# Fused linear attention and MLP on one core: loads of a pair's first sets reordered, attention steps of two shapes side by side, ranks laid out anew

## Chip, cores and metric

The kernel runs on one core of one Trainium2 chip. Times are device microseconds (us) of that core for one execution of the whole program. All engines of the core work on it: PE (matmuls), PEld (its weight loads), DVE, ACT, POOL and SP, whose queue issues nearly all DMAs in order.

## What is computed

```python
def phi(x):                       # random features of a row, 128 of them
    h = np.einsum('bhsd,md->bhsm', x, omega) - np.sum(x*x, -1, keepdims=True)/2
    return np.exp(h - np.max(h, -1, keepdims=True)) / np.sqrt(m)
q_p, k_p = phi(q*scale), phi(k*scale)
kv  = einsum('bhsm,bhsd->bhmd', k_p, v);  z = sum(k_p, axis=2)
num = einsum('bhsm,bhmd->bhsd', q_p, kv); den = einsum('bhsm,bhm->bhs', q_p, z)[..., None] + 1e-06
x   = (num/den) as [8, 576, 512]          # 8 batches, 8 heads of 64, 576 rows
xn  = (x - mean)/sqrt(var + 1e-06) * g_ln
out = x + np.maximum(xn @ w_ch1, 0) @ w_ch2   # 512 -> 2048 -> 512
```

## The kernel before

**Tiles.** The 4608 rows of x are 36 chunks of 128 (`c`), and four chunks make a tile of 512 rows (`t`, 9 of them). The MLP of tiles 0 to 2 (`NREG`) is done tile by tile (`mm1` L1073 to L1075, `mm2` L1116 to L1118). Tiles 3 to 8 are done in three pairs (`gen_pair`, p = 0, 1, 2): the two tiles of a pair are the halves of one larger product that is computed with 7 products where 8 would be needed (`one_set`, products of `product` at L1374 to L1376). Each float32 product is made of three matmuls of 128x512 on high and low parts; such a matmul is called a wide matmul below.

**A pair** has four groups. A group is two sets of 7 products (`one_set(p, j)`, j = 0 to 7; one product is 6 wide matmuls) and then 8 chunks of the second layer (`one_chunk`, L1466 to L1468, 12 wide matmuls each). The seven left-hand forms of the activations (`gen_forms`, names `A11, S3, S2, A12, S1, A22, S4`, products 0 to 6) are made once per pair by ACT (L1292) and DVE (L1295, L1302) from the transposed, normalized x of both tiles. The forms of pairs 1 and 2 go into the buffers of the pair before, which come free in its last set.

**Loads of a pair,** all from DRAM by SP's queue: the weights of each product, 256 KB (`gen_slot`, L1343, a ring of 8 slots `w<-wf`; product m's slot is filled again for product m + 8); the second layer's weights, 512 KB for each of 16 f, four buffers (`gen_w2`, L1359, `w<-w2a`); and the pair's 8 chunks of x for the residual, 256 KB each (`gen_back`, L933, `x<-away`), to which each chunk's result is added (`drain`, L1485). Finished chunks are stored by L1148.

**Attention** runs between the MLP's matmuls, ahead of the tiles that need it. A step holds a pair of PSUM banks and is one of three shapes: "row" steps, K = 64, 8 matmuls of 64x128 or 2 of 64x512 (keys L651, early queries L812); "col" steps, 16 matmuls onto 64 columns (sums of keys and values L714, numerators L895); "all" steps, which have the MLP's own shape (later queries L829, L830). Row and col steps are called narrow. Between two wide matmuls there can be a visit of one or more narrow steps. After L895 a chunk of x is normalized (L906, L979), split (L996), transposed by a DMA (L999) and copied to the pair's forms' source.

**Order.** The whole order of work is written out by a planner (`Plan`) that keeps a modelled clock for each engine. Every generator part has a rank; among parts that can start, the lowest rank goes first. `serve` decides at each wide matmul whether a visit is made. With `lend` (between chunks and between sets) it looks for two narrow steps of the same shape, which then go back to back on two bank pairs; a third may join as a guest. A single narrow step is taken when its rank has fallen below `plan.at`, the rank of the MLP's present place, or when it has waited for over `PATIENCE`. If the MLP itself is blocked, any visit is made (`run`). `EARLIER` gives the attention of each tile its rank, `WF` that of the weights' forms and their stores, `SHIFT` moves single parts.

Of the kernel before, what the change touches and what calls it, by code (L numbers as in the profile page):

```python
# [39 lines left out]
TC = T // P  # L40
NREG = 3
# [32 lines left out]
class Plan:  # L74
# [14 lines left out]
    FILL, IDLE = 10000, 20000  # L89
    HOLDER = 100  # L90
    LENT = 1500
    SWITCH = 0.37
    PATIENCE = 50.0
    PEEK, AHEAD, TILL = {ACT: 0.1, DVE: 0.1, PE: 0.1}, 5, 60.0
    BIAS = {PE: 0.0, ACT: 0.2, DVE: 0.5, POOL: -0.2, SP: 0.0}
# [3 lines left out]
    def __init__(self):  # L99
        self.free_at = dict.fromkeys((PE, ACT, DVE, POOL, SP), 0.0)  # L100
        self.dma_at, self.landed = 0.0, [0.0] * Plan.QUEUE
        self.lock, self.two_at = (0.0, 0.0), 0.0
        self.free_at[SP] = 0.74
        self.ready = []
        self.blocked = []
        self.made = {}
        self.places = {}
        self.cur = None
        self.count = 0
        self.visits = []  # L110
        self.mlp = None
        self.pair, self.loan, self.at = (), (), 0
        self.shared = {}

    def add(self, rank, gen):
# [76 lines left out]
    def serve(self, lend):  # L192
# [6 lines left out]
        if lend and len(narrow) > 1 and self.open(self.loan):  # L199
            pairs = [(a, b) for i, a in enumerate(narrow) for b in narrow[i + 1 :] if a.want[1] == b.want[1]]  # L200
            if pairs:
                a, b = pairs[0]
                guests = [p for p in narrow if p not in (a, b) and p.want[1] == a.want[1] == "col" and p.want[3]]
                if not guests and a.want[1] == "col":
                    third = [p for p in narrow if p not in (a, b) and p.want[1] == "col"]
                    if third and b.want[3]:
                        b, guests = third[0], [b]
                    elif third and a.want[3]:
                        a, guests = third[0], [a]
                if guests:  # L210
                    self.lodge(guests[0])
                    self.go(b, self.loan, b.want[2])
                    self.go(a, self.pair, a.want[2])
                    return True
                self.go(b, self.loan, Plan.SWITCH + b.want[2])
                self.go(a, self.pair, a.want[2])
                return True
        for p in waiting:
            if p.want[1] == "all":
                if len(narrow) < 2:  # L220
                    self.go(p, self.pair, p.want[2])
                    return False
            elif p.rank < self.at or now - p.ready(PE) > Plan.PATIENCE:
                self.go(p, self.pair, Plan.SWITCH + p.want[2])
                return False
        return False
# [85 lines left out]
def favor_ffn(ctx, tc, kT, kTr, vF, vR, qT, qD, omT, gT, w1, w2, out):  # L312
# [1042 lines left out]
    def gen_w2(p, f, t_w):  # L1355
        w = tile_of(t_w, [P, 2, DM], F32R)
        yield wait("w2", f)
        yield dma(2 * P * DM)
        nc.sync.dma_start(f32(w), w2_away[f])  # L1359
        w2s[p, f] = t_w, w  # L1360
        done(("w2s", p, f))
# [18 lines left out]

    def one_set(p, j):

        ta, f, g = NREG + 2 * p, 2 * j, 2 * j + 1
        b_a, b_d = b_h
        b_b, b_c = b_acc[0:2] if j % 2 == 0 else b_acc[1::-1]
        sk = snaps[j % 2]
        yield "get", (b_a,)
        yield from product(p, j, 0, b_a, True)
        plan.add(MOST_URGENT, gen_copy(p, j, b_a, b_b))
        yield "get", (b_d,)  # L1390
        yield from product(p, j, 1, b_d, True)
        yield wait("a2b", p, j)
        yield from product(p, j, 2, b_b, False)
        plan.add(MOST_URGENT, gen_snap(p, j, b_b, sk[0], 0))
        plan.add(MOST_URGENT, gen_x2(p, j, b_c, b_d, sk[0]))
        yield from product(p, j, 3, b_a, False)
        plan.add(MOST_URGENT, relu2(ta, f, bank(b_a), b_a))
        yield wait("snap", p, j, 0)
        yield from product(p, j, 4, b_b, False)
        plan.add(MOST_URGENT, gen_snap(p, j, b_b, sk[1], 1))  # L1400
        plan.add(MOST_URGENT, gen_y2(p, j, b_d, sk[1], ta + 1, g))
        yield wait("x2", p, j)
        yield from product(p, j, 5, b_c, False)
        plan.add(MOST_URGENT, relu2(ta + 1, f, bank(b_c), b_c))
        yield wait("snap", p, j, 1)
        yield from product(p, j, 6, b_b, False)
        plan.add(MOST_URGENT, relu2(ta, g, bank(b_b), b_b))

    def gen_copy(p, j, b_a, b_b):
# [87 lines left out]
    def gen_pair(p):  # L1497
        ta = NREG + 2 * p
        if not snaps:
            for i in range(2):  # L1500
# [3 lines left out]
                for k in range(2):  # L1504
                    extra[snaps[i][k]] = two_[:, k]
                    free(snaps[i][k])
        for c in range(ta * TC, (ta + 2) * TC):
            plan.add(URGENT, gen_back(c))
        for gr in range(NF // 4):
            for s in range(2):  # L1510
                plan.at = NS * ta + 16 * gr + 4 * s
                yield from one_set(p, 2 * gr + s)
            for c in range(2 * TC):
                plan.at = NS * ta + 16 * gr + 8 + c
                if 0 < c < 2 * TC - 1:
                    yield us(PE, 0.0)
                    plan.serve(True)
# [69 lines left out]
    for p in range(NPAIR):  # L1587
        plan.add(URGENT, gen_stage(p))
        plan.add(URGENT, gen_forms(p))
        plan.add(URGENT, gen_ring(p))  # L1590
        plan.add(URGENT, gen_ring2(p))
    plan.add(LAST, gen_mlp())
    plan.add(Plan.IDLE, gen_warm())
    plan.run()


SHIFT = {}
LINE = 16
SPILL, BACK, OPEN = 0, NF - 2, 6
FLIP = 1  # L1600
LASTCUT = 320
HALVES = 2
EARLIER = {2: 1.6, 3: 2.1, 4: 2.4, 5: 3.9, 6: 4.4, 7: 5.8, 8: 6.4}
VLATE = 0
COLS = 16
SUMS, TAIL, ONES = -200, 1, DVE
# [4 lines left out]
QF = 2 * TC  # L1611
EARLY, BEFORE = 1, ("x", 3)
FORMS = ("x", 7)
WF = (30, 4)
GATE_K, GATE_Q = 3, 3
WARM, COLD = 0.0, 5.0
RW, RS = -10, 0.5
# [43 lines left out]
```

## Time and profile before

| | us |
|---|---|
| median of 3 timed runs | 964.18 (961.55 to 966.34) |
| the profiled execution, own time | 959.42 |
| its span, first to last instruction | 957.6 |
| PE busy in the span | 938.7 |
| DVE busy | 590.8 |
| ACT busy | 462.5 |
| POOL busy | 118.6 |
| chain that ended last: PE, DVE, DMA, ACT | 73%, 9%, 9%, 4% |

The mean granted clock of TensorE is 0.997. In the rows below matmuls overlap: the duration of one is longer than the distance to the next start, so the distances between starts are what adds up. "xN" counts instructions merged in a row; a float32 matmul of the narrow shapes counts as two, so that a col step is x32 and a row step of keys x16.

### The profile page before, as it was taken

Reading aid. Unit: us, or ns where it says so; the run is one execution under the profiler, and the core shown is the slowest. Engines: PE = TensorE matmul, PEld = TensorE weight load, DVE = VectorE, ACT = ScalarE, POOL = GpSimd, SP = SyncE. Lnnn points to the kernel's source line nnn. Section 1 sums busy time; section 2 is a strip of 40 time slices with the busy share of each in tenths; the row PEclk is TensorE's granted clock in tenths of the full one; section 3 lists DMA queues with packets and bytes.
Section 4 is the critical chain, followed back from the end, with each engine's and each line's share of the span. In section 5 each row is a group of like instructions: output and inputs, shape, how many; then the busy total and the mean of one; then the engine's idle time right before and its main releaser. Section 6 shows DMA issues by size and latency. Waiting matters only on the chain.

```text
span 957.6 us, 16656 instructions
## 1 busy us (share of the span) xinstructions
PE 938.7 (98%) x6587; PEld 760.6 (79%) x6587; DVE 590.8 (62%) x990; ACT 462.5 (48%) x847; POOL 118.6 (12%) x47
## 2 busy tenths in 40 slices
PE   8999999999999999999999999899999998999998
PEld 6877787788787878888887888787877887888887
DVE  6999997694468977374755658365444563242342
ACT  6888884466555664354645455344252423022130
POOL 5003102011140440001210410041010000000000
PEclk9999999999999999999999999999999999999999
DMA  8576499964367486676549084936372638345242
GB/s 301 204 260 254 140 314 381 377 204 116 101 185 251 137 258 207 225 234 201 163 149 303 34 254 160 312 100 230 93 232 84 230 127 301 114 129 181 61 154 88
DMA packets 124030, 187.98 MB, mean 196 GB/s; under 512 B 42800, under 2 KB 61616, under 8 KB 123952
## 3 DMA queue, kind: packets, MB, share of 16 engines
q1 hardware_dynamic: 123808, 186.66, 59.5%
q8 instruction: 52, 0.85, 0.3%
q10 hardware_dynamic: 144, 0.26, 0.1%
q14 instruction: 26, 0.21, 0.1%
HBM read 134.45 MB, written 44.04 MB: 186 GB/s over the span
## 4 chain that ended last, share of the span: by engine, by line
PE 73%; DVE 9%; DMA 9%; ACT 4%; issue 4%; POOL 1%; SPq 0%; DVEq 0%; ACTq 0%; POOLq 0%
PE b L1466 8%; PE b L1468 8%; PE b L1467 8%; PE b L1374 6%; PE b L1376 5%; PE b L1375 5%; PE b L1116 4%; PE b L714 4%; PE b L1073 3%; PE b L1118 3%; PE b L1117 3%; PE b L1075 3%; PE b L1074 3%; DMA wide<-wide 3%; PE b L651 3%
## 5 line engine op out<-in xcount | busy, mean ns | idle before, releaser
L841 POOL PARTITION_ALL_REDUCE quad<-quad x34 | 112.4, 3330 | 584.6 <-ACT quad L357 516.3
L1466 PE MATMUL b<-w,w 128*128 128x512 f32 (+1 forms) x388 | 152.4, 393 | 0.3 <-ACT w L1441 0.3
L1468 PE MATMUL b<-w,w 128*128 128x512 f32 (+1 forms) x388 | 150.7, 388 | 0.2 <-DVE w L1443 0.2
L1467 PE MATMUL b<-w,w 128*128 128x512 f32 (+1 forms) x388 | 150.4, 388 | 0.0
L1374 PE MATMUL b<-w,w 128*128 128x512 f32 x336 | 133.8, 398 | 8.2 <-DMA w<-wf 5.6
L1375 PE MATMUL b<-w,w 128*128 128x512 f32 x336 | 131.5, 391 | 0.0
L1376 PE MATMUL b<-w,w 128*128 128x512 f32 x336 | 131.4, 391 | 0.0
L1468 PEld LDWEIGHTS b<-w,w 128*128 128x128 f32 x388 | 72.9, 188 | 16.2 <-DVE w L1443 0.8
L1466 PEld LDWEIGHTS b<-w,w 128*128 128x128 f32 x388 | 72.9, 188 | 16.2 <-ACT w L1441 0.7
L660 ACT ACTIVATE kp<-b,mb 128x128 f32<-128x128 f32 x256 | 70.9, 389 | 29.4 <-DVE mb L654 27.8
L1467 PEld LDWEIGHTS b<-w,w 128*128 128x128 f32 x388 | 72.9, 188 | 14.3
L1374 PEld LDWEIGHTS b<-w,w 128*128 128x128 f32 x336 | 63.5, 189 | 25.8 <-issue 6.4
L1485 DVE SCALAR_TENSOR_TENSOR x<-b,st,x 128x512 f32<-128x512 f32 (+2 forms) x53 | 39.1, 739 | 68.5 <-PE b L1468 68.3
L1073 PE MATMUL b<-xnT,w 128*128 128x512 f32 (+1 forms) x200 | 78.6, 393 | 0.5 <-ACT kp L660 0.5
L1116 PE MATMUL b<-w,hid 128*128 128x512 f32 x192 | 78.2, 407 | 0.0
L1075 PE MATMUL b<-xnT,w 128*128 128x512 f32 (+1 forms) x200 | 76.5, 382 | 0.5 <-DVE xnT L1049 0.4
L1074 PE MATMUL b<-xnT,w 128*128 128x512 f32 (+1 forms) x200 | 76.3, 381 | 0.0
L1118 PE MATMUL b<-w,hid 128*128 128x512 f32 x192 | 75.3, 392 | 0.6 <-DVE hid L1091 0.5
L1117 PE MATMUL b<-w,hid 128*128 128x512 f32 x192 | 75.0, 391 | 0.0
L1376 PEld LDWEIGHTS b<-w,w 128*128 128x128 f32 x336 | 63.4, 189 | 13.5
L1375 PEld LDWEIGHTS b<-w,w 128*128 128x128 f32 x336 | 63.5, 189 | 12.5
L1443 DVE SCALAR_TENSOR_TENSOR w<-b,w 128x512 fp32r<-128x512 f32 x72 | 49.5, 688 | 29.5 <-ACT w L1441 28.4
(159 smaller groups left out, 1527.7 us busy)
## 6 DMA issues: line engine op xcount, KB each, us to landing
w<-wf SPq DMA_DIRECT2D x168, 256.0 KB, 3.4
w<-w2a SPq DMA_DIRECT2D x48, 512.0 KB, 5.2
w<-w SPq DMA_DIRECT2D x32, 512.0 KB, 6.2
quad<-qD SPq DMA_DIRECT2D x28, 512.0 KB, 4.6
w2a<-w SPq DMA_DIRECT2D x16, 512.0 KB, 6.2
wf<-wide SPq DMA_DIRECT2D x32, 256.0 KB, 2.7
away<-x SPq DMA_DIRECT2D x29, 256.0 KB, 2.8
v<-vF SPq DMA_DIRECT2D x28, 260.0 KB, 3.3
```

The costliest lines, as they stand in the source:

```text
L841: nc.gpsimd.partition_all_reduce(mx.rearrange("p a b -> p (a b)"), qc.rearrange("p a b -> p (a b)"), P, bass_isa.ReduceOp.max)
L1073: nc.tensor.matmul(ph[:, ts], w[:, 0, cs], xnT[:, 0, k, ts], start=k + i0 == 0, stop=False)
L1074: nc.tensor.matmul(ph[:, ts], w[:, 1, cs], xnT[:, 0, k, ts], start=False, stop=False)
L1075: nc.tensor.matmul(ph[:, ts], w[:, 0, cs], xnT[:, 1, k, ts], start=False, stop=k == NK - 1 and i1 == TC)
L1116: nc.tensor.matmul(accs[i][:, c], hl[:, 0, cs], w[:, 0, c], start=(f == 0), stop=False)
L1118: nc.tensor.matmul(accs[i][:, c], hl[:, 1, cs], w[:, 0, c], start=False, stop=f == NF - 1 and c == parts[-1])
L1374: nc.tensor.matmul(o, w[:, 0, cs], hi[:, k], start=first and k == 0, stop=False, skip_group_check=True)
L1375: nc.tensor.matmul(o, w[:, 1, cs], hi[:, k], start=False, stop=False, skip_group_check=True)
L1376: nc.tensor.matmul(o, w[:, 0, cs], lo[:, k], start=False, stop=k == 1, skip_group_check=True)
L1466: nc.tensor.matmul(acc[:, o], hl[:, 0, cs], w[:, 0, o], start=n == 0 and o is parts[0], stop=False)
L1467: nc.tensor.matmul(acc[:, o], hl[:, 0, cs], w[:, 1, o], start=False, stop=False)
L1468: nc.tensor.matmul(acc[:, o], hl[:, 1, cs], w[:, 0, o], start=False, stop=n == 3 and o is parts[-1])
```

## The change

```diff
@@ Plan
-    SWITCH = 0.37
+    SWITCH, TURN = 0.37, 0.1
-        self.pair, self.loan, self.at = (), (), 0
+        self.pair, self.loan, self.at, self.where = (), (), 0, 0
@@ Plan.serve, after no two steps of one shape were found
+            if MIXED:
+                a, b = narrow[0:2]
+                self.go(b, self.loan, Plan.SWITCH + b.want[2])
+                self.go(a, self.pair, Plan.TURN + a.want[2])
+                return True
...
-            elif p.rank < self.at or now - p.ready(PE) > Plan.PATIENCE:
+            elif p.rank + WAIT[self.where] < self.at or now - p.ready(PE) > Plan.PATIENCE:
@@ gen_w2
         yield wait("w2", f)
+        yield wait("go2", p, f)
         yield dma(2 * P * DM)
@@ one_set
+        due = list(range((NREG + 2 * p) * TC, (NREG + 2 * p + 2) * TC)) if j == 1 else []
+        def tick(q):
+            if q in GO2 and j % 2 == 0:
+                done(("go2", p, 2 * j + GO2.index(q)))
+            for _ in range(2 if q == 0 else 1):
+                if due:
+                    plan.add(URGENT, gen_back(due.pop(0)))
         yield from product(p, j, 0, b_a, True)
+        tick(0)
...
         yield from product(p, j, 6, b_b, False)
+        tick(6)
@@ gen_pair
-        for c in range(ta * TC, (ta + 2) * TC):
-            plan.add(URGENT, gen_back(c))
...
-                plan.at = NS * ta + 16 * gr + 4 * s
+                plan.at, plan.where = NS * ta + 16 * gr + 4 * s, 1
-                plan.at = NS * ta + 16 * gr + 8 + c
+                plan.at, plan.where = NS * ta + 16 * gr + 8 + c, 2
@@
-        plan.add(URGENT, gen_ring(p))
+        plan.add(URGENT - 500, gen_ring(p))
-SHIFT = {}
+SHIFT = {('gen_var', 16): 2, ('gen_w2store', 13): 2, ('gen_q', 26): 16}
+WAIT = (0, 0, 4)
+MIXED = True
+GO2 = 0, 2, 4, 6
-EARLIER = {2: 1.6, 3: 2.1, 4: 2.4, 5: 3.9, 6: 4.4, 7: 5.8, 8: 6.4}
+EARLIER = {2: 1.8, 3: 2.25, 4: 2.4, 5: 3.95, 6: 4.85, 7: 5.6, 8: 6.8}
-WF = (30, 4)
+WF = (52, 4)
```

The slots' loads get a lower rank than the other loads. The four loads of second-layer weights of a group are asked for after products 0, 2, 4 and 6 of its first set; the 8 loads of x after the products of a pair's second set, two after the first of them and one after each of the rest. No matmul, no vector operation and no load is added or taken away: PE's order has 5051 matmuls in both. In the changed kernel the lines between the planner and `gen_w2` stand 5 further down; L1374 is L1380, L1466 is L1488, L1343 is L1348, L1359 is L1365, L933 is L938.

In the order of PE's instructions, in the first layer of tile 1 and near there, the narrow steps stand as follows before (names: `v`, `kp` of a sum of keys, `kv`, `quad` of a numerator, the rest is the MLP):

```order
L1075 MATMUL b<-xnT_1868,w_20_686 128x512
L714 MATMUL b<-v_1903,kp_1926 64x65 x16
L1073 MATMUL b<-xnT_1868,w_20_686 128x512
L1074 MATMUL b<-xnT_1868,w_20_686 128x512
L1075 MATMUL b<-xnT_1868,w_20_686 128x512
L1116 MATMUL b<-w_10_676,hid_2048 128x512
L1117 MATMUL b<-w_10_676,hid_2048 128x512
L1118 MATMUL b<-w_10_676,hid_2048 128x512
L895 MATMUL b<-kv_401,quad_1953 64x65 x16
```

and the same sums and numerator in the changed kernel:

```order
L1123 MATMUL b<-w_10_676,hid_2031 128x512
L719 MATMUL b<-v_1976,kp_1998 64x65 x16
L900 MATMUL b<-kv_401,quad_1843 64x65 x16
L719 MATMUL b<-v_1975,kp_1998 64x65 x16
L1121 MATMUL b<-w_20_730,hid_2096 128x512
```

Three visits with wide matmuls between them (the third stands 6 wide matmuls ahead of the rows shown) are one visit. From the first wide matmul on, PE's order has these visits:

| visit | before | changed |
|---|---|---|
| one col step | 29 | 17 |
| one row step of keys | 20 | 9 |
| two col steps | 14 | 10 |
| two row steps | 5 | 10 |
| three col steps | 3 | 8 |
| four col steps | 0 | 1 |
| a row step and a col step | 0 | 1 |
| with queries of 64x512 | 4 | 4 |
| all | 75 | 60 |

On SP's queue, at the start of pair 1 (`w2a` the second layer's weights, `away` the chunks of x, `wf` the products' weights), there stand before:

```order
L1359 DMA w_120_6191<-w2a_100 128x1024
L933 DMA w_150_4331<-away_4595 128x512
L933 DMA x_6192<-away_4579 128x512
L933 DMA x_6193<-away_4773 128x512
L933 DMA x_6194<-away_4937 128x512
L933 DMA w_140_4315<-away_5291 128x512
L933 DMA x_6195<-away_5357 128x512
L933 DMA x_6196<-away_5473 128x512
L933 DMA x_6212<-away_5727 128x512
L1343 DMA w_00_3406<-wf_90 128x512 x2
L1343 DMA w_10_3500<-wf_90 128x512 x2
```

and in the changed kernel:

```order
L1348 DMA w_00_3364<-wf_90 128x512
L1365 DMA w_100_6217<-w2a_97 128x1024
L1348 DMA w_00_3364<-wf_90 128x512
L1348 DMA w_10_3420<-wf_90 128x512
L1365 DMA w_120_6223<-w2a_98 128x1024
L1348 DMA w_10_3420<-wf_90 128x512
L1348 DMA w_20_3508<-wf_90 128x512
L1365 DMA w_110_6230<-w2a_99 128x1024
L1348 DMA w_20_3508<-wf_90 128x512
L1348 DMA w_110_4122<-wf_91 128x512
L1365 DMA w_120_6234<-w2a_100 128x1024
L1348 DMA w_110_4122<-wf_91 128x512
```

Before, four loads of `w2a` (the last is shown) and eight of `away` stand ahead of the first slot of the pair, that for product 8; now the slots come first, with a load of `w2a` behind each second one, and the loads of `away` follow in the second set, one behind each slot.

On PE, in the first set of pair 0, the products 5 (`w_90`) and 6 (form S4, `w_100`) stand before next to each other:

```order
L1374 MATMUL b<-w_90_4221,w_20_3560 128x512
L1375 MATMUL b<-w_90_4221,w_20_3560 128x512
L1376 MATMUL b<-w_80_4222,w_20_3560 128x512
L1374 MATMUL b<-w_100_4271,w_110_4042 128x512
L1375 MATMUL b<-w_100_4271,w_110_4042 128x512
```

and in the changed kernel a visit of two col steps (16 rows, the first two are shown) stands between them:

```order
L1380 MATMUL b<-w_90_4309,w_20_3508 128x512
L1381 MATMUL b<-w_90_4309,w_20_3508 128x512
L1382 MATMUL b<-w_80_4310,w_20_3508 128x512
L719 MATMUL b<-v_3375,kp_3912 64x65 x2
L719 MATMUL b<-v_3911,kp_3941 64x65 x2
```

The attention moves to later places: counted in wide matmuls from the first, the last numerator of pair 0's tiles (chunk 19) stands at 966 before and 996 now, of pair 1 (chunk 27) at 1689 and 1758, of pair 2 (chunk 35) at 2316 and 2457. The pairs start at 1176, 1896 and 2616 in both.

## Rows read from the trace of the kernel before

**Rows 1.** Page, part 1: busy us, share of span, instructions.

```profile
PE 938.7 (98%) x6587; PEld 760.6 (79%) x6587; DVE 590.8 (62%) x990; ACT 462.5 (48%) x847; POOL 118.6 (12%) x47
```

**Rows 2.** Waits of PE, whole span, first and last of thirteen: us, times, longest.

```profile
PE b L1374 <- DMA w<-wf: 5.6, 2, 3.0
...
PE b L1468 <- DVE w L1443: 0.2, 1, 0.2
```

**Rows 3.** Timeline of PE, one col step: start us, duration, line, operation, shapes.

```profile
510.92 0.39 PE L1376 MATMUL b<-w,w 128*128 128x512 f32 x1
511.24 1.15 PE L895 MATMUL b<-kv,quad 128*64 128x65 f32 x32
...
512.66 0.39 PE L1375 MATMUL b<-w,w 128*128 128x512 f32 x1
```

**Rows 4.** Timeline of PE, two col steps.

```profile
476.70 2.08 PE L714 MATMUL b<-v,kp 128*64 128x65 f32 x64
...
479.05 0.39 PE L1467 MATMUL b<-w,w 128*128 128x512 f32 x1
```

**Rows 5.** Timeline of PE, two row steps, then elsewhere one row step.

```profile
422.38 2.06 PE L651 MATMUL b<-om,wide 64*128 64x128 f32 x32
...
424.70 0.39 PE L1467 MATMUL b<-w,w 128*128 128x512 f32 x1
...
521.36 1.16 PE L651 MATMUL b<-om,wide 64*128 64x128 f32 x16
...
522.79 0.39 PE L1375 MATMUL b<-w,w 128*128 128x512 f32 x1
```

**Rows 6.** Timeline of PE ahead of the MLP: shapes side by side.

```profile
24.92 1.16 PE L782 MATMUL b<-w,w 64*128 64x128 f32 x16
26.01 1.15 PE L895 MATMUL b<-kv,quad 128*64 128x65 f32 x32
26.99 1.10 PE L714 MATMUL b<-w,w 128*64 128x65 f32 x32
```

**Rows 7.** Timeline of PE, first product of pair 1's second set.

```profile
611.87 0.40 PE L1376 MATMUL b<-w,w 128*128 128x512 f32 x1
615.25 0.77 PE L1374 MATMUL b<-w,w 128*128 128x512 f32 x1 [2.98 <-DMA w<-wf]
...
618.28 0.39 PE L1375 MATMUL b<-w,w 128*128 128x512 f32 x1
```

**Rows 8.** Timeline of SP's queue at pair 1's start.

```profile
599.21 0.92 SPq L1359 DMA_DIRECT2D w<-w2a  x2
...
607.60 2.04 SPq L933 DMA_DIRECT2D x<-away  x3
610.01 19.46 SPq L1343 DMA_DIRECT2D w<-wf  x14
```

**Rows 9.** Busy time by stretch there; then PEclk, DMA share, GB/s.

```profile
615.00:619.00 4.00, 3.75 (x13) 2.80 (x15) 0.00 (x0) 0.37 (x2) 0.00 (x0) 0.61 1.06 408
```

**Rows 10.** Timeline of PE, the same place of pair 2.

```profile
795.72 0.39 PE L1376 MATMUL b<-w,w 128*128 128x512 f32 x1
...
797.76 0.39 PE L1376 MATMUL b<-w,w 128*128 128x512 f32 x1
800.81 0.47 PE L1374 MATMUL b<-w,w 128*128 128x512 f32 x1 [2.66 <-DMA w<-wf]
801.11 0.40 PE L1375 MATMUL b<-w,w 128*128 128x512 f32 x1
```

**Rows 11.** Page, part 6: DMA issues of a slot, KB each, us to landing.

```profile
w<-wf SPq DMA_DIRECT2D x168, 256.0 KB, 3.4
```

**Rows 12.** Timelines of PE and DVE: pair 0's last numerator, last form, start.

```profile
335.44 1.15 PE L895 MATMUL b<-kv,quad 128*64 128x65 f32 x32
...
388.04 0.68 DVE L1295 TENSOR_TENSOR w<-w,w 128x512 fp32r<-128x512 f32 x1
...
393.30 0.39 PE L1374 MATMUL b<-w,w 128*128 128x512 f32 x1
```

More of the change, by code (lines that the diff above doesn't have):

```diff
@@ L1391, in one_set @@
         yield from product(p, j, 1, b_d, True)
+        tick(1)
         yield wait("a2b", p, j)
         yield from product(p, j, 2, b_b, False)
+        tick(2)
         plan.add(MOST_URGENT, gen_snap(p, j, b_b, sk[0], 0))
@@ L1396, in one_set @@
         yield from product(p, j, 3, b_a, False)
+        tick(3)
         plan.add(MOST_URGENT, relu2(ta, f, bank(b_a), b_a))
@@ L1399, in one_set @@
         yield from product(p, j, 4, b_b, False)
+        tick(4)
         plan.add(MOST_URGENT, gen_snap(p, j, b_b, sk[1], 1))
@@ L1403, in one_set @@
         yield from product(p, j, 5, b_c, False)
+        tick(5)
         plan.add(MOST_URGENT, relu2(ta + 1, f, bank(b_c), b_c))
```

## Prediction

> **What bounds the kernel now.** I read the page's busy times first: PE is busy for 938.7 of 957.6 us [rows 1], no other engine comes near, so a change helps only where it makes PE's own sequence shorter or closes a hole in it. The two kernels give PE the same matmuls, so the work itself cancels. What is left is, first, the holes, from the waits of PE [rows 2]: thirteen rows, of which the loads of a pair's weights (`w<-wf`) are the largest, 5.6 us in only two waits; the other twelve add up to 8.9 us in small pieces, of which 2.4 lie ahead of the MLP. Second, time that counts as busy and still isn't work: what it costs to leave the wide matmuls for a visit of narrow steps and to come back. That doesn't stand in a wait. It shows in the distances between starts in PE's timeline [rows 3 to 6], and in those of wide matmuls alone, which are 2.04 us for 9, so 0.227 each [rows 10].
>
> **Visits, removed and merged.** One col step: from the last wide start to the visit's start 0.32 us, from there to the second wide start after it 1.42 [rows 3]; two wide distances (0.454) would have passed anyway, so the visit costs 1.29. With two col steps the second part is 2.35 [rows 4], 0.93 more. So a col step is 0.93 and its visit adds 0.36. Row steps: 1.43 for one, 2.32 for two [rows 5], so 0.89 a step and, with the same 0.32 ahead, 0.41 a visit. The steps are the same in number in both kernels, so only the visits count: col visits fall from 46 to 36, row visits from 25 to 19 (the four with queries of 64x512, the same in both, left aside), and one visit has both shapes (all counted in the two orders). That gives 10 x 0.36 + 6 x 0.41 = 6.1 us less. The mixed visit costs one overhead, about 0.38, plus the turn between its shapes. Ahead of the MLP such turns are there: from a row step to a col step 1.09 us pass, from a col step to a col step 0.98 [rows 6], so a turn is about 0.1. Against 6.1 stands 0.5, **5.6 us gained**. I take the whole of it, since these steps stand on PE and nothing runs beside them there. What they lose if the cover is gone: two steps that come together hand ACT and DVE twice the work at once, and with ACT late PE waits for hidden values, in waits of the size that is there now (the smallest kind in [rows 2] is 0.2 us). Of the three edits (`MIXED`, `WAIT`, new ranks) I do not split the gain; two shapes meet only once, so most of it comes from later ranks and from single steps that wait for a partner.
>
> **Loads at a pair's start.** In pair 1 the first product of the second set starts 3.38 us after the wide start before it, 3.15 too late, and the next seven starts take 3.03 us where 1.59 would do, 1.44 too long [rows 7]; there the granted clock is 0.61 on average over 4 us [rows 9], so part of the time at the lower of the two levels, right after PE had stood still. In pair 2 the same place is 2.82 late, and 0.07 in the next start, with no such slow stretch [rows 10]. Together **7.5 us**. The cause stands on SP's queue: slot 8 came free with the first product of the pair, at about 601 us (42 wide matmuls and a visit ahead of the hole at 611.87), but its load is issued at 610.0, behind four loads of `w2a` and eight of `away` [rows 8]; these 4.2 MB take 10.3 us at 408 GB/s [rows 9]. The change puts the slot's load first, so it can be issued 8.7 us sooner, and a slot's load lands 3.4 us after its issue [rows 11]. The slot's product is 7 products, 42 x 0.227 = 9.5 us, after it came free. So the wait goes, with some 6 us to spare, and I count all 7.5 as gained.
>
> What is moved with it: SP's queue holds the same loads, in another order. Behind a slot's load, which waits for its product on PE, there now stand `w2a`, `away`, attention's loads and DMA transposes; such a wait is 1.36 us (one product) at most when PE runs, and these need not be on time to a microsecond: the first chunk needs its `w2a` after another whole set, and the load of x is needed only by `drain`, whose bank is asked for two chunks later. Pair 0 doesn't wait at this place in the old order, so nothing is gained there.
>
> **Forms, the new late thing.** All attention moves back, and the forms of a pair need its last chunk of x. In pair 0 the last numerator starts at 335.4, the last half of form S4 ends at 388.7 (53.3 us later), and the pair starts at 393.3 [rows 12]; S4 is wanted 36 wide matmuls later still, at 401.5. In the new order 216 wide matmuls lie between that numerator and S4's product, 49.0 us, and with four "all" matmuls twice (1.8) and three visits (3.2, 2.2 and 2.2) 58.4 us. Against a chain of 53.3 that is 5 us to spare instead of 13, and the visit that the planner puts right ahead of S4's product shows that it saw the form come last. No row shows this chain when it is pressed; between nothing (the chain as it was) and 2 us (ACT and DVE lag as they do behind PE's small waits) I take 0.5, near the first. In pairs 1 and 2 138 and 159 wide matmuls are left, 31 us and 36 us, and more with visits; the first form needs far less than the seventh, so I take 0 there, up to 1 each.
>
> **The rest.** `WF` and `SHIFT` move the making of the weights' forms and a few attention parts among work that PE covers; the small waits of [rows 2] will stand in other places. The 6.5 us of them in the MLP could be half or one and a half of that, so 3 us each way, and I take no change.
>
> **Sum,** against the profiled execution's own 959.4: -5.6 - 7.5 + 0.5 gives 946.8. The median of the timed runs is 964.2, 4.8 above that execution; I carry the difference over and get **951.6 us**.
>
> **Rivals.**
> 1. *The wait at the pair's start only moves.* Loads of 0.5 MB now stand between the slots; if a later slot, a `w2a` or a form makes PE wait for as long, the visits' gain alone is left: 964.2 - 5.6 = 958.6. For it: the bytes are the same. Against it: PE waits for one slot only, the first, and all later slots of the set were on time behind it. Chance 0.09.
> 2. *The visits' gain is eaten by ACT and DVE.* Merged steps bring their work in lumps, and PE waits for `hid` or for forms instead: 964.2 - 7.5 + 0.5 = 957.2; with both rivals half true it is much the same. Against it: DVE is at 62%, ACT at 48% [rows 1]. Chance 0.09.
> 3. *Forms late at all three pairs.* If the chain is slower under pressure by 5 to 8 us beyond what is to spare, each pair starts with a wait of that kind: 3 x 4 = 12 us, which gives 963.6, no change. For it: the slack falls in every pair. Chance 0.07.
> 4. *Slower: DMA can't carry the spread loads.* In the first set of each of a pair's groups, 7 slots and 4 loads of `w2a` are 3.93 MB in 7 x 1.36 = 9.5 us, 412 GB/s, where the trace's highest over 4 us is 408 [rows 9]. A slot has 9.5 us and needs 3.4 [rows 11], so up to 6 us of delay is hidden: it decides once the rate in such a set falls below 3.93 MB in 15.5 us, 253 GB/s. At 230 GB/s a set would take 17.1 us and wait 1.6, twelve times 19 us: with 13.1 gained, 970. Against it: the rate in the old burst was far above that. Chance 0.03.
>
> The Trainium skill, in "DMA: Bandwidth & Descriptors", section "Where 436 GB/s comes from", holds that transfers between HBM and SBUF are bound at about 358 GB/s per core. The 408 GB/s of [rows 9] disagrees, and the measurement decides; by the page's figure a set's loads would take an estimated 11.0 us, 1.5 late, still inside what is hidden, so it would not bring about the fourth case either.
>
> **How the numbers follow.** The forecast has 0.72, with its own range of 947 to 957 (3 us of small waits, 2 of forms, and the timed runs' own spread of some 2). Adding rivals 1 and 2 the range is 945.5 to 960 and leaves out the third and the fourth, and tails. A measurement can tell about 0.5% from no change, 4.8 us: below 959.4 counts as faster. The forecast, rival 2 and most of rival 1 lie there, 0.87 less something for a before that is measured anew: 0.85. Within 0.5%: rival 3, the rest of rival 1, some of the forecast's tail, 0.11. Slower: rival 4 and one like it that I don't see, 0.04.
>
> **What would show it.** PE's row `w<-wf` gone from its waits, and slot loads on SP's queue issued within a product of their release; no stretch with a lower clock at a pair's second set; 60 visits with the distances of [rows 3 to 5]; no wait of over 2 us at products 0 to 6 of a pair's first set. I am wrong if PE's waits hold a new row of over 3 us, above all for a form (DVE L1300), a `w2a` or a slot later than the first, or if the sum of PE's small waits has grown by as much as the visits gave.

## The result, and the profile after

| | before | changed |
|---|---|---|
| median beside each other, us | 964.76 (961.55 to 966.34, 4 runs) | 949.51 (947.88 to 951.27, 4 runs) |
| changed / before | | 0.9846, 95% interval 0.9814 to 0.9879 |
| the profiled execution, own time | 959.42 | 950.52 |
| its span | 957.6 | 948.7 |

The forecast was 951.6 us, with a range of 945.5 to 960. The kernel is faster by 15.3 us between the medians, by 8.9 between the two profiled executions. In a second job the changed kernel had 947.59 (944.78 to 949.85) beside a before of 961.16, a ratio of 0.9855 (0.9829 to 0.9882). Four jobs gave before 964.8, 961.2, 961.8 and 961.9, so the gain is nearer to 14 us than to 15.

The page, part 1 (busy us, share of the span, instructions), the answer to [rows 1]:

```profile
PE 932.1 (98%) x6587; PEld 761.0 (80%) x6587; DVE 593.8 (63%) x991; ACT 466.4 (49%) x850; POOL 118.9 (13%) x47
```

The waits of PE over the whole span (us, times, longest), the answer to [rows 2], the three largest and the smallest:

```profile
PE b L1121 <- ACT hid L1094: 2.6, 1, 2.6
PE b L1380 <- ACT hid L1440: 2.1, 2, 1.3
PE b L817 <- ACT kp L682: 1.5, 1, 1.5
...
PE b L834 <- ACT quad L362: 0.2, 1, 0.2
```

No row is left in which PE waits for `w<-wf`; on top stands a wait that the kernel before didn't have, for hidden values in the tile-by-tile part.

PE's timeline (start us, duration, line) at product 8 of pair 1, from 615.90 on, the answer to [rows 7] (counted again, the old hole stood there too, at the second product of the second set, not at the first as I wrote):

```profile
615.67 0.39 PE L1382 MATMUL b<-w,w 128*128 128x512 f32 x1
615.90 0.39 PE L1380 MATMUL b<-w,w 128*128 128x512 f32 x1
...
617.48 0.39 PE L1381 MATMUL b<-w,w 128*128 128x512 f32 x1
```

The first start follows after 0.23 us where it took 3.38, and the next seven take 1.58 us where they took 3.03. SP's queue ahead of it, the answer to [rows 8], and the page's line on a slot's load, the answer to [rows 11]:

```profile
606.46 0.34 SPq L1153 DMA_DIRECT2D out<-x  x1
606.89 0.38 SPq L1348 DMA_DIRECT2D w<-wf  x1
607.32 0.45 SPq L1365 DMA_DIRECT2D w<-w2a  x1
607.87 1.72 SPq L1348 DMA_DIRECT2D w<-wf  x2
```

```profile
w<-wf SPq DMA_DIRECT2D x168, 256.0 KB, 4.3
```

The pair starts at 603.05, so its first slot is asked for 3.8 us later, where before it was 10.1 (599.90 to 610.01). Of the 3.8 us 2.6 pass until the slot is free, since four matmuls of queries now stand inside the pair's first product, and 1.3 behind a transpose and a store of a finished chunk (`out<-x`) on the queue. From product 8 of a pair on, every other slot is asked for within 1 us of its release. A slot's load lands 4.3 us after its issue, no longer 3.4: in the runs below it is 3.5 to 3.7 where second-layer loads aren't spread among the slots, and 4.1 to 4.7 where they are (6.3 in e10, with twice that traffic). Taken slot by slot from the landings, products 8 to 13 of the pairs now find their slots there 3.6 to 8.4 us early. Before, product 8 of pairs 1 and 2 waited, and pair 0, which I had called free of the hole, escaped it by 0.2 us (product 9).

The one mixed visit, in PE's timeline, with its neighbours:

```profile
534.54 0.39 PE L1490 MATMUL b<-w,w 128*128 128x512 f32 x1
534.86 1.16 PE L656 MATMUL b<-om,wide 64*128 64x128 f32 x16
535.95 1.15 PE L900 MATMUL b<-kv,quad 128*64 128x65 f32 x32
...
537.38 0.40 PE L1489 MATMUL b<-w,w 128*128 128x512 f32 x1
```

The turn from the row step to the col step starts 1.09 us after the row step, as in [rows 6]; counted to the second wide start behind it the visit costs 2.38 us.

Two sums are used from here on, both from PE's timeline: the **visits' sum** (for each visit the time from the last wide start ahead of it to the second wide start behind it, less 0.454) and the **holes** (what the other distances between wide starts take beyond 0.227). Visits went from 121.7 to 116.8 us, holes from 19.0 to 15.0, together the 8.9 us of the span. The two pair-start holes (7.5) are gone, so all the other holes grew by 3.5. More than that is one place, in tile 2. PE's timeline there, then ACT's, then DVE's and POOL's:

```profile
353.95 0.39 PE L1080 MATMUL b<-xnT,w 128*128 128x512 f32 x1
356.97 0.50 PE L1121 MATMUL b<-w,hid 128*128 128x512 f32 x1 [2.63 <-ACT hid L1094]
...
358.13 0.63 PE L1121 MATMUL b<-w,hid 128*128 128x512 f32 x1
358.55 0.63 PE L1122 MATMUL b<-w,hid 128*128 128x512 f32 x1
```

```profile
354.20 0.20 ACT L960 ACTIVATE st<-st 128x4 f32<-128x4 f32 x1 [3.64 <-DVE wide L1192]
354.31 1.03 ACT L827 CAST quad<-quad 128x1024 fp32r<-128x1024 f32 x1
355.38 1.04 ACT L1001 COPY wide<-wide 128x1024 uint16<-128x1024 uint16 x1
356.33 0.59 ACT L1094 ACTIVATE hid<-b 128x512 fp32r<-128x512 f32 x1
```

```profile
351.00 1.89 DVE L364 CAST wide<-wide 128x512 fp32r<-128x512 f32 x1 [2.19 <-issue]
...
352.81 1.36 DVE L956 TENSOR_SCALAR st<-st 128x4 f32<-128x4 f32 x1
352.92 1.25 DVE L1192 TENSOR_TENSOR wide<-wide,wide 128x512 fp32r<-128x512 f32 x1
```

```profile
350.71 3.43 POOL L846 PARTITION_ALL_REDUCE quad<-quad  x1 [11.01 <-ACT quad L362]
```

Read from the bottom: beside POOL's all-reduce DVE's cast takes 1.89 us (0.42 elsewhere), what stands behind it on DVE comes late, ACT waits 3.64 us for a tiny statistic, and the hidden values queue on ACT behind it and two copies. PE stands for 2.63 us, and then wide starts come 0.43 us apart instead of 0.23, eight in a row: over 356.9 to 361.2 the granted clock is 0.62.

```profile
356.90:361.20 4.30, 4.23 (x11) 3.02 (x12) 2.81 (x7) 2.50 (x5) 0.00 (x0) 0.62 0.28 65
```

Wait and slow starts together cost 4.8 us (353.95 to 361.45 is 7.50 us for twelve distances, 2.72 of them due).

### The profile page after: what moved, and what is told of

Read it like the earlier page. It is cut to its first block, busy times and chain, and to the rows that moved or that the text cites. A ratio compares the mean times of both kernels' runs of the same rounds, so it can differ in the third digit from the quotient of the medians.

```text
span 948.7 us, 16592 instructions
## 1 busy us (share of the span) xinstructions
PE 932.1 (98%) x6587; PEld 761.0 (80%) x6587; DVE 593.8 (63%) x991; ACT 466.4 (49%) x850; POOL 118.9 (13%) x47
## 4 chain that ended last, share of the span: by engine, by line
PE 78%; DVE 10%; DMA 6%; ACT 3%; issue 2%; SPq 1%; DVEq 0%; ACTq 0%
PE b L1488 9%; PE b L1490 9%; PE b L1489 9%; PE b L1380 7%; PE b L1381 7%; PE b L1382 7%; PE b L1121 3%; PE b L1078 3%; PE b L656 3%; PE b L1080 3%; PE b L1123 3%; PE b L1079 3%; PE b L1122 3%; PE b L719 3%; PE b L900 2%
## 5 line engine op out<-in xcount | busy, mean ns | idle before, releaser
L1488 PE MATMUL b<-w,w 128*128 128x512 f32 (+1 forms) x388 | 151.6, 391 | 0.0
L1380 PE MATMUL b<-w,w 128*128 128x512 f32 x336 | 131.9, 393 | 2.1 <-ACT hid L1440 2.1
L1507 DVE SCALAR_TENSOR_TENSOR x<-b,st,x 128x512 f32<-128x512 f32 (+2 forms) x57 | 42.1, 740 | 73.7 <-PE b L1490 73.3
L1490 PEld LDWEIGHTS b<-w,w 128*128 128x128 f32 x388 | 72.9, 188 | 16.6 <-DVE w L1465 1.6
L1488 PEld LDWEIGHTS b<-w,w 128*128 128x128 f32 x388 | 72.8, 188 | 15.7 <-DVE x L1507 0.2
L1380 PEld LDWEIGHTS b<-w,w 128*128 128x128 f32 x336 | 63.1, 188 | 16.6 <-ACT hid L1440 3.2
L1382 PEld LDWEIGHTS b<-w,w 128*128 128x128 f32 x336 | 63.1, 188 | 13.3
```

Source lines behind the costliest of these rows:

```text
L1380: nc.tensor.matmul(o, w[:, 0, cs], hi[:, k], start=first and k == 0, stop=False, skip_group_check=True)
L1382: nc.tensor.matmul(o, w[:, 0, cs], lo[:, k], start=False, stop=k == 1, skip_group_check=True)
L1488: nc.tensor.matmul(acc[:, o], hl[:, 0, cs], w[:, 0, o], start=n == 0 and o is parts[0], stop=False)
L1490: nc.tensor.matmul(acc[:, o], hl[:, 1, cs], w[:, 0, o], start=False, stop=n == 3 and o is parts[-1])
```

## The experiments

All runs but one in one table; times are medians, "before" is the kernel before on the same chip in the same job, the sums are from each run's profiled execution. "Slots first" says whether the slots' loads have the lower rank.

| run | slots first | visits | us / before | ratio (95%) | visits' sum | holes |
|---|---|---|---|---|---|---|
| before, profiled | no | 75 | | | 121.7 | 19.0 |
| e1 | yes | 75 | 953.66 / 961.93 | 0.9923 (0.9904 to 0.9941) | 123.5 | 13.1 |
| e2 | yes | 72 | 955.07 / 961.93 | 0.9943 (0.9925 to 0.9962) | 122.3 | 16.8 |
| e3 | no | 63 | 962.66 / 961.93 | 1.0011 (0.9992 to 1.003) | 120.5 | 24.1 |
| e4 | yes | 62 | 952.26 / 961.93 | 0.9907 (0.9885 to 0.9928) | 119.7 | 13.9 |
| e5, the changed kernel | yes | 60 | 947.59 / 961.16 | 0.9855 (0.9829 to 0.9882) | 116.8 | 13.7 |
| e6 | yes | 63 | 956.27 / 961.16 | 0.9949 (0.993 to 0.9968) | 121.4 | 16.6 |
| e8 | yes | 66 | 954.31 / 961.16 | 0.9925 (0.9896 to 0.9953) | 121.0 | 15.9 |
| e9 | yes | 60 | 954.07 / 961.82 | 0.9923 (0.9897 to 0.9949) | 119.6 | 17.7 |
| e10 | yes | 60 | 969.07 / 961.82 | 1.0087 (1.0058 to 1.0116) | 119.4 | 36.5 |
| e11 | yes | 62 | 952.97 / 961.82 | 0.9918 (0.9891 to 0.9945) | 119.3 | 14.8 |
| e12 | yes | 61 | 954.53 / 961.82 | 0.9927 (0.9899 to 0.9954) | 119.6 | 13.3 |

Span less visits' sum less holes is 816.1 to 816.9 us in all but e10, so the two sums account for the spans (in e10 it is 819.3: PE waits 2.9 us more as the MLP begins, outside both sums). A profiled execution can lie some us from its kernel's median (e12's own time is 951.07, its median 954.53; e10's 977.01, its median 969.07).

**One part alone: slots first (e1).** The kernel before, with one number changed.

```diff
-        plan.add(URGENT, gen_ring(p))
+        plan.add(URGENT - 500, gen_ring(p))
```

> The kernel before with one edit: the slots' loads get the lower rank (URGENT - 500); second-layer weights and chunks of x are asked for as before, visits as before (75). My theory (a pair's first slots stand too late on SP's queue): both holes at the second set of pairs 1 and 2 close, 7.5 us of the profiled run and perhaps more of the timed ones, ratio 0.992 to 0.988, no wait on a slot of over 1 us. Rival (the same bytes at the same place only move the wait, the spreading is what counts): the wait stays or moves to a chunk of x or to second-layer weights, ratio over 0.996.

8.3 us faster. The waits of PE in e1, first and last rows:

```profile
PE b L1374 <- ACT hid L1418: 2.6, 4, 1.0
...
PE b L1468 <- DVE w L1443: 0.2, 1, 0.2
```

The row `w<-wf` that led [rows 2] is gone, and holes fell by 5.9 us. PE's order is that of the kernel before up to wide matmul 1953, just behind the place of [rows 7]. So the cause given for [rows 7, 10] is shown: the slot's load stood behind others on SP's queue. No spreading is needed for it.

**The load part and the attention part (e2, e3).** e2 is the changed kernel with the planner numbers of before, e3 the changed kernel with the loads of before.

```diff
e2:
-SHIFT = {('gen_var', 16): 2, ('gen_w2store', 13): 2, ('gen_q', 26): 16}
-WAIT = (0, 0, 4)
-MIXED = True
+SHIFT = {}
+WAIT = (0, 0, 0)
+MIXED = False
...
-EARLIER = {2: 1.8, 3: 2.25, 4: 2.4, 5: 3.95, 6: 4.85, 7: 5.6, 8: 6.8}
+EARLIER = {2: 1.6, 3: 2.1, 4: 2.4, 5: 3.9, 6: 4.4, 7: 5.8, 8: 6.4}
...
-WF = (52, 4)
+WF = (30, 4)
e3:
-        yield wait("go2", p, f)
...
-        due = list(range((NREG + 2 * p) * TC, (NREG + 2 * p + 2) * TC)) if j == 1 else []
+        due = []
...
+        for c in range(ta * TC, (ta + 2) * TC):
+            plan.add(URGENT, gen_back(c))
...
-        plan.add(URGENT - 500, gen_ring(p))
+        plan.add(URGENT, gen_ring(p))
```

> The changed kernel with the planner's rules and numbers of before (no MIXED, WAIT 0, old EARLIER, WF and SHIFT), so that only the loads are reordered and spread; 72 visits. My theory: as e1, 7.5 us and three visits (1.1 us), ratio 0.990 to 0.986. Rival (visits carry the gain): ratio over 0.995. If spreading adds something to the rank, e2 is faster than e1 by over 1 us beside the three visits.

> The changed kernel with the loads as before, so that only the planner's rules and numbers for the attention are changed; 63 visits. My theory: 12 visits fewer are worth 12 x 0.37 = 4.4 us, and the holes at the second sets of pairs 1 and 2 stay, ratio 0.994 to 0.997. Rival (merged steps bring ACT and DVE late, so nothing is left): ratio 0.998 to 1.002. Other rival (the attention's new places free DMA at the pairs' starts too): ratio below 0.991.

e2 gains 6.9 us, no more than e1: spreading adds nothing there, and the ratio that I expected is missed. e3, with 12 visits fewer than before, gains nothing, against my theory. Waits of PE in e3, the first three rows, and its timeline at pair 2's second set:

```profile
PE b L1379 <- ACT hid L1439: 5.7, 5, 1.7
PE b L1379 <- DMA w<-wf: 3.7, 1, 3.7
PE b L1121 <- ACT hid L1094: 1.9, 1, 1.9
```

```profile
797.44 0.39 PE L1381 MATMUL b<-w,w 128*128 128x512 f32 x1
801.50 0.77 PE L1379 MATMUL b<-w,w 128*128 128x512 f32 x1 [3.67 <-DMA w<-wf]
802.07 0.63 PE L1380 MATMUL b<-w,w 128*128 128x512 f32 x1
...
806.76 0.53 PE L1379 MATMUL b<-w,w 128*128 128x512 f32 x1
```

The pair-start hole is 3.83 us too long, and the next twelve starts take 5.26 us where 2.72 would do; this place alone costs 6.4 us, nearly as much as the two did. (Pair 1 has no such hole in e3: all four second-layer loads, where before it was three, had gone out before the pair began, and the first slot is asked for at 606.63.) Waits for `hid` in the pairs grew from 1.5 us before to 5.7. Twelve visits should be worth 4.6 us; their sum fell by 1.2, since some visits last longer (3.5 us for two col steps at 554.4, where 2.2 is usual).

**Slots first and the attention part, nothing spread (e6).** e3 with the lower rank for the slots.

```diff
-        plan.add(URGENT, gen_ring(p))
+        plan.add(URGENT - 500, gen_ring(p))
```

> e3 (attention as in the changed kernel's rules, loads as before) with one edit more: the slots' loads get the lower rank, as in e1; second-layer weights and chunks of x are asked for as before, so nothing is spread; 63 visits. Theory (the rank closes the holes, the spread adds nothing): equal to the changed kernel (e5) within 2 us, and the two parts add: e1's 8 us plus the 4 us of 12 visits, ratio 0.986 to 0.989. Rival (the spread is needed): 4 us or more slower than e5, with a wait on second-layer weights, chunks of x or a slot at a pair's start.

> The changed kernel as it is, so that it stands on one chip and beside one set of runs of before with the next three. Each half alone gave little of the whole (e2 6.9 us, e3 nothing). If the halves need each other, the ratio stays near 0.985; if part of the first result was the chip, it comes out at 0.988 or more.

e6 is 4.9 us faster than before, e5 13.6. PE's order in e6 is that of e3 to the matmul, so the rank alone is worth some 6 us here too (ratios 1.0011 and 0.9949). The theory that the parts add has fallen: slots first alone gave 8.3, slots and loads 6.9, the attention part nothing, slots and attention 4.9, and all of it 13.6. In the difference of e6 and e5, 7.7 us of span, visits hold 4.6 (of which three more visits are 1.1) and holes 2.9.

**The spread, halved (e11, e12).** In e11 second-layer loads are no longer spread, in e12 the loads of x.

```diff
e11:
-        yield wait("go2", p, f)
e12:
-        due = list(range((NREG + 2 * p) * TC, (NREG + 2 * p + 2) * TC)) if j == 1 else []
+        due = []
...
+        for c in range(ta * TC, (ta + 2) * TC):
+            plan.add(URGENT, gen_back(c))
```

> Changed kernel, but the four loads of second-layer weights of a group are asked for as soon as a buffer is free, as before; the loads of x are still spread over a pair's second set and the slots still go first. 62 visits (60 in the changed kernel, 63 where nothing is spread); PE's order is that of the changed kernel up to wide matmul 1752. Nothing spread at all gave 956.3, the changed kernel 947.6. Theory A (it is the order of the loads that is worth 8.7 us): one of the two halves carries it, so this and the next run lie at 948 and 956, in one order or the other. Theory B (spreading only makes the planner lay out attention's steps anew, and each layout has its own sum of small waits): the visits' part is 2 x 0.4 = 0.8 us, and the time lies at 952 +- 4 with no w<-wf in PE's waits; the difference to the changed kernel stands in the holes at narrow steps and hid, not at loads.

> Changed kernel, but the eight loads of x are asked for at a pair's start, as before; the second-layer weights are still spread over a first set and the slots still go first. 61 visits; PE's order is that of the changed kernel up to wide matmul 1992. Theory A (order of the loads): 948 if the run before lies at 956, and the other way round. Theory B (layout of attention's steps): one visit more is 0.4 us, and since the order is the same up to the middle of pair 1, the time at wide matmul 1908 is that of the changed kernel within 1.5 us; the end at 950 +- 4, the difference made behind wide matmul 1992.

953.0 and 954.5: neither is at 948, so no half of the spread carries the 8.7 us alone. They aren't clearly apart from e6's 956 either, since the intervals overlap; that the two halves are worth something only together isn't excluded by these times. Theory B fits better: e4 and e8 below have the whole spread and lie at 952 and 954 all the same, and PE waits for slots neither in e11 nor in e12 (at most 0.3 us). PE's order in e12 is the changed kernel's up to wide matmul 1992, and its time is near: wide matmul 1990 starts at 625.1 us in e12, at 624.7 in e5. Behind it e12 loses 2.2 us more by its end. These two executions differ by 2.6 us where the medians differ by 6.9, so most of the difference between the medians has no place shown.

**Two planner rules (e4, e8).**

```diff
e4:
-MIXED = True
+MIXED = False
e8:
-WAIT = (0, 0, 4)
+WAIT = (0, 0, 0)
```

> The changed kernel with MIXED off: 62 visits, two more than the changed kernel, no visit of two shapes. My theory: within 1.5 us of the changed kernel, ratio to before 0.983 to 0.987: two shapes side by side are worth next to nothing by themselves. Rival (the rule is what lets the planner merge): 4 us or more slower than the changed kernel, ratio 0.989 or more.

> The changed kernel with WAIT at 0, so that a single narrow step goes between chunks as soon as its rank is due: 66 visits in place of 60. Theory: 6 x 0.37 = 2.2 us slower than e5. Rival (the small waits of PE outweigh such a difference, since each order has its own): anywhere within 4 us of e5, with the sum of holes different by more than the sum of visits.

Without `MIXED` the time rises by some 4.7 us, without `WAIT` by 6.7, far more than 2 and 6 visits at 0.4 us and more than I expected of either. Against e5 the visits' sum is 2.9 and 4.2 us larger, the holes 0.2 and 2.2: most of it is visits that last longer than their steps; that data comes late there is my reading, and no run changed it by itself.

**No pairing at all (e7).** Each narrow step alone, 82 visits.

```diff
-        if lend and len(narrow) > 1 and self.open(self.loan):
+        if False and lend and len(narrow) > 1 and self.open(self.loan):
```

> The changed kernel with the planner forbidden to make visits of several steps between chunks and sets: 82 visits in place of 60, the same narrow steps, the loads as changed. It doubles the cost in dispute, the price of a visit. Theory (a visit costs PE 0.36 to 0.41 us of its own): 22 x 0.37 = 8.1 us slower than e5. Rival (a visit's price is hidden, since PE would have waited for ACT and DVE anyway, and merging only makes those waits longer): 3 us or less slower than e5, with the visits' sum in the timeline grown by 8 us and PE's other holes shrunk by 5 or more.

1015.88 us beside a before of 961.16, a ratio of 1.0571 (1.0541 to 1.06): 68 us above the changed kernel, where 22 visits are worth some 8. Two rows of its PE timeline:

```profile
403.54 2.08 PE L656 MATMUL b<-om,wide 64*128 64x128 f32 x16 [3.53 <-ACT quad L362]
411.54 2.08 PE L656 MATMUL b<-om,wide 64*128 64x128 f32 x16 [1.10 <-ACT quad L362]
```

The second row begins a visit of 19.8 us, the visits' sum is 176.3 us, 59.5 more than in e5, and the row step takes 2.08 us where 1.16 is usual: the mean granted clock is 0.969. My reading is that attention, taken singly, falls behind the MLP until it is on the path itself, so that pairing is worth more than its visits because it keeps attention ahead. My theory of 8.1 us is far off, and this run can't serve to price a visit.

**The hole in tile 2 (e9).** One copy that stands on ACT ahead of the late hidden values is held until they are made.

```diff
         halves = tile_of(t_p, [P, 2, DM], U16)
+        if (t, i) == (4, 3):
+            yield wait("hid", 2, 9)
```

> Changed kernel; the copy ahead of one transpose (tile 4, chunk 3, on ACT) is held until the hidden values of tile 2, f = 9 are made. ACT's order there is then: that step's relu first, the copy behind it. PE's order keeps 60 visits; up to wide matmul 1212 it is the same, later one step moves from a visit to another. In both profiled executions of the changed kernel PE waits there at 355.5 to 357 for hid (1.9 and 2.6 us), and some 8 to 10 starts after it are 0.2 us too long. Theory A (the relu is late because the copy stands ahead of it on ACT, and the copy waits for its buffer): the wait goes, with the slow starts behind it, 3.5 to 4.7 us, so 947.6 - 4 = 943.6 us, and PE's waits hold no row for hid over 1.5 us there. Rival B (the relu is late because ACT stands behind DVE and POOL, whatever its order): the wait stays at 1.5 us or more, 947 +- 1.5 us. Rival C (the gain comes back as other waits in the new order of the later stages): no hid wait at 356, but the sum of holes and of the waits inside visits is as large as before, 947 +- 2.

6.5 us slower than e5, where theory A wanted 4 us less. ACT and PE at the place:

```profile
354.51 0.20 ACT L960 ACTIVATE st<-st 128x4 f32<-128x4 f32 x1 [3.64 <-DVE wide L1194]
354.63 1.03 ACT L827 CAST quad<-quad 128x1024 fp32r<-128x1024 f32 x1
355.56 0.20 ACT L962 ACTIVATE st<-st 128x4 f32<-128x4 f32 x1
355.67 0.57 ACT L1096 ACTIVATE hid<-b 128x512 fp32r<-128x512 f32 x1
```

```profile
356.29 0.50 PE L1123 MATMUL b<-w,hid 128*128 128x512 f32 x1 [1.54 <-ACT hid L1096]
...
358.58 0.80 PE L1125 MATMUL b<-w,hid 128*128 128x512 f32 x1 [1.56 <-DVE hid L1098]
```

The hidden values come 0.66 us sooner (355.67 against 356.33) and no more, since ACT still waits 3.64 us for DVE; their second half, on DVE behind statistics and a 1.22 us subtraction, brings a second wait. So in this execution rival B holds on the cause, ACT behind DVE beside POOL, and C on the rest: in pair 0 a new wait of 1.7 us and a longer visit (4.57 us where 3.15 is usual) follow. But the last link isn't always the same. In the second traced execution of the changed kernel (e5) DVE has no such cast beside the all-reduce, and the same hole (1.87 us) ends with that very copy, which waits 1.69 us for a transfer; in e3 and e8 too ACT waits there for transfers, in e11 3.64 us for DVE. The hole is there with 1.5 to 2.9 us in every run with the new ranks and pairing, and in none with the ranks of before, so it comes with the new ranks; no run takes the all-reduce away from the place.

**Twice the second-layer traffic (e10).** Behind each load the queue copies the same 512 KB from DRAM to DRAM; nobody reads it, and PE's order is unchanged.

```diff
         nc.sync.dma_start(f32(w), w2_away[f])
+        nc.sync.dma_start(dram.tile([P, 2, DM], F32, tag=f"spare{f}", name=f"spare{f}", bufs=1), w2_away[f])
```

> Changed kernel; behind each of the 48 loads of second-layer weights SP's queue issues a copy of the same 512 KB from DRAM to DRAM that nobody reads. PE's order is the same to the row. It presses the rival of loads that DMA can't carry: a group's first set then has 7 slots and 4 + 4 pieces of 512 KB, 6.0 MB, where a set takes 9.5 us. In the profiled changed kernel the slots of a second set land 3.5 to 8 us before their product. At some 400 GB/s 6.0 MB take 15.1 us, 5.6 us longer than the set. Theory A (rate at 400 GB/s holds, slots late by their place in the set): the last slots of the second sets come up to 2 us late, in most of 12 sets, with some slow starts behind: 958 us (952 to 972), with a row w<-wf of 8 to 20 us in PE's waits. Rival B (there is more to spare than the landings say): no row w<-wf, 947.6 +- 2. Rival C (transfers of all queues slow each other below 300 GB/s): 20 us for a set, 5 or more late in each of 12, over 1000 us.

969.07, so the 25 MB cost some 22 us against the changed kernel (1.0087 against 0.9855). The time is that of theory A, the place isn't. Waits of PE, the first two rows and that for slots, then one row of ACT:

```profile
PE b L1381 <- ACT hid L1441: 7.5, 4, 3.6
PE b L834 <- DVE quad L829: 6.9, 3, 4.2
...
PE b L1381 <- DMA w<-wf: 0.2, 1, 0.2
```

```profile
650.10 1.04 ACT L827 CAST quad<-quad 128x1024 fp32r<-128x1024 f32 x1 [5.59 <-DMA quad<-qD]
```

The slots land 0.1 us early at worst (3.5 without the copies): they go first. What comes late is what queues behind them, queries (5.59 us in that row) and transposes, and through ACT the hidden values.

## Why the prediction came out right, step by step

- **Pair starts, 7.5 us: right, shown.** The row is gone, and the rank alone gave 8.3 us (e1). Loads are issued within a product of their release, as forecast (1.3 us at most). The spare is 3.6 to 8.4 us where some 6 was worked out: in pair 2, where the first slot goes out 0.03 us after its release and lands 3.3 us later, it is 6.0, and it is smaller where landing takes longer.
- **Visits, 5.6 us: the size right in this order, the reason too simple.** Their sum fell by 4.9 us, one col visit takes 1.28, one row visit 1.29, and four col steps 4.08, as the distances of [rows 3 to 5] said. But I took all of it as a property of the number of visits. It isn't: e9 has 60 visits as well and a sum of 119.6, and e1 with its 75 takes no longer than e9. Seven other layouts with slots first (e2, e4, e6, e8, e9, e11, e12), with 60 to 72 visits lie within 952.3 to 956.3, without a trend, and e1 among them. The changed layout, 947.6, is 5 to 9 us below all of them. So the mechanism of rival 2, PE waiting for what ACT and DVE bring late, is no rare case: by their medians the neighbours show next to nothing of the visits' gain beside e1, in most of their traces more time is lost inside visits and at hidden values, and the changed order is the one in which they took least. Why this one isn't shown. Its numbers (`SHIFT`, `EARLIER`, `WF`) were the same in most of these neighbours and may suit this one combination; no run sets them anew for another, so a neighbour with numbers of its own is a rival left untested. That the forecast took the visits' gain whole and got it was in part luck.
- **Form S4 of pair 0, 0.5 us: nothing was lost.** The last half of the form ends at 402.49, 58.5 us after its numerator (53.3 before), and its product starts at 404.99. Without the visit put ahead of it the product would have come 0.4 us after the form.

```profile
401.81 0.68 DVE L1300 TENSOR_TENSOR w<-w,w 128x512 fp32r<-128x512 f32 x1
```

```profile
402.97 2.09 PE L719 MATMUL b<-v,kp 128*64 128x65 f32 x64
404.99 0.50 PE L1380 MATMUL b<-w,w 128*128 128x512 f32 x1
```

- **Small waits, no change within 3 us: mis-sized.** Holes apart from the pair starts grew from 11.5 to 15.0 us, with 4.8 in tile 2 alone, and a good part of that isn't wait but slow starts behind it, which I had priced at pair 1's start and nowhere else. In e5 the holes are 13.7, 2.2 more and inside my 3 us. The forecast's own sign of being wrong, a new row of over 3 us, came near with 2.6.
- **From one execution to the median, 4.8 us carried over: wrong.** The profiled execution of the changed kernel lies 1.0 us above its median, not 4.8 below. Against its own time the sum was 946.8, and 950.5 came; the two errors, +3.7 and -5.8, have opposite signs, and that is how 951.6 met 949.5. Executions of the kernel before spread over 957 to 966 us. In which stage those differ from the profiled one isn't known, since only that one was traced. The mean granted clock of each execution gives a hint: of 48 executions of the kernel before, the 20 with 0.998 or more have a median of 959.4 us, the 8 with 0.995 or less 964.0, and the changed kernel's ten all have 0.998 or more. So slow starts as at pair 1's second set [rows 7] may be more or fewer from one execution to the next, and part of why the medians gained more than the traced spans; at no place is it shown.
- **Rivals.** The first and the third are excluded (no wait for slots, `w2a` or forms). The fourth needs twice the traffic, and comes then by another road (e10); the 408 GB/s that I took there for the trace's highest over 4 us isn't that, over 13 to 17 us it is 422. What `SHIFT` and `WF` do by themselves wasn't run.

## What to carry to other kernels

A hole that a transfer leaves on the bounding engine, with its queue read back to what stands ahead, was here a gain that could be counted on: one rank was worth over half of the whole. Time saved on that engine by laying out other work anew was only an upper bound, since each new order has small waits of its own, and orders that differ by a few visits scattered by several us. Such a term belongs in a prediction with that scatter as its error, and a change of this kind is better kept or dropped by timing than by its count of visits.

## What the hardware showed that I had not expected

DVE beside POOL's all-reduce: a cast of 0.42 us took 1.89, in e9 2.06, and in e12, where the cast had got through, the 0.2 us operation behind it took 1.86.

```profile
350.79 0.41 DVE L364 CAST wide<-wide 128x512 fp32r<-128x512 f32 x1 [1.23 <-issue]
...
351.12 1.86 DVE L956 TENSOR_SCALAR st<-st 128x4 f32<-128x4 f32 x1
352.89 0.68 DVE L1192 TENSOR_TENSOR wide<-wide,wide 128x512 fp32r<-128x512 f32 x1
```

```profile
350.87 3.41 POOL L846 PARTITION_ALL_REDUCE quad<-quad  x1 [10.42 <-ACT quad L362]
```

In all three the first blocked instruction ends 2.1 to 2.2 us after the all-reduce began, though that lasts 3.4. What follows isn't the same: in e12 the subtraction behind it takes 0.68 us, as elsewhere (0.69 in e5), but in the changed kernel and in e9 the statistic behind the cast takes 1.36 us and ends with the all-reduce (354.17 and 354.14 us in the changed kernel). The Trainium skill, "SBUF — State Buffer", section "SBUF: two separate sides", holds that the pair of ports which DVE and GpSimd share goes for a whole instruction to whichever starts first, for certain forms of DVE's instructions. These rows agree that DVE is shut out; they also show DVE instructions coming through while the profile's one record of the all-reduce still runs, and no run shows what the all-reduce holds at which time.

A wait of PE is dearer than its row. Behind 2.63 us in tile 2 eight starts came 0.2 us late each, behind 3.67 in e3 twelve, the granted clock in such a stretch being a mixture of its two levels (0.62 over 4.3 us). In the kernel before the hole at a pair's second set had that tail in pair 1, behind 2.98 us [rows 7], and none in pair 2, behind 2.66 [rows 10].
